# Small attention products placed crosswise in the PE array, chunk 1's tiles moved, and the third triangular solve spread over two passes

## The chip, the cores and the metric

The kernel runs on one NeuronCore of a Trainium2 chip. The metric is the device time of one execution in microseconds; the median of several runs counts. TensorE (PE in the profile) multiplies, VectorE (DVE) and ScalarE (ACT) do elementwise work and empty PSUM, GpSimd (POOL) and SyncE (SP) issue most DMAs.

## The reference

Inputs are q, k, v of shape (4, 8, 768, 48) and beta of shape (4, 8, 768), with a chain of three blocks, cut here to what is computed:

```python
k_n = k / (np.linalg.norm(k, axis=-1, keepdims=True) + 1e-06)
for t in range(S):                       # S = 768, state is 48 x 48 for each of 32 heads
    y[:, :, t] = np.einsum('bhd,bhde->bhe', q[:, :, t], state)
    v_old = np.einsum('bhde,bhd->bhe', state, kt)
    state = state + bt * np.einsum('bhd,bhe->bhde', kt, vt - v_old)
x = y.transpose(0, 2, 1, 3).reshape(3072, 384)
h = np.maximum(x @ w_in, 0.0);  x = h * h @ w_out           # w_in 384 x 2048
h = np.maximum(np.maximum(x @ w1, x @ w2), x @ w3)          # each 384 x 768
return h @ w_out2                                           # 768 x 384
```

## The kernel before

The recurrence is worked in 12 chunks of 64 tokens (C = 64). A chunk's state updates become products with the inverse X of a 64 x 64 triangular matrix for every head. The 32 heads stand as 16 pairs u; the two heads t of a pair lie in partitions 0 to 63 and 64 to 127, and the pairs fall into two halves p of 8 (U2). A product of one head contracts over its 48 or 64 partitions and writes 64 partitions, so it occupies one quarter of the array: its row half is where its inputs lie, its column half where its output lies. `half(t)` as output of head t is a diagonal quarter, `half(1 - t)` a crosswise one. In float32 one matmul of the code is two instructions in the trace.

Work of one chunk c, in `attention(c)`, is a generator whose steps are: `load_x` (X's 32 x 32 blocks into the tile xb), `scaled` and `aa` (v times a norm, pA = keys x state Sb, v -= pA), `zz` and `ww` (pZ, pW: the off-diagonal block of X), `uu` (pU = X v, copied to u), `st2` for each half (pD = state growth, pY = queries x old state plus masked products p x u, then the state is added to and pY copied to yy), and `st3` (transposes pT into X, the MoE's input). `load_att(c + 1)` issues the next chunk's DMAs on POOL: keys and queries (the tile kqs, called big in the trace), v, ktp, p. The 32 x 32 blocks are inverted for two chunks at a time by `solve32(g)`, 30 steps of two VectorE instructions each (L291, L292); the first three solves belong to chunks 0 and 1, 2 and 3, 4 and 5. `kkps` makes the products kk and p that a later solve and chunk need.

The program has a prologue (chunks 0 and 1, the first solve, the conversion of the first 12 weight tiles), six passes of the first MoE (`moe_a(P)`, chunks 2P and 2P + 1), and the second MoE. In pass P, `steps` runs 32 steps of MoE work, each a group of nine float32r products (p at L576, px at L592), and between them the steps of other generators. Lists of step numbers say when: `attention(2)` in pass 0 with [13, 13, 15, 17, ...] takes its first two steps at step 13. TensorE and VectorE keep the order in which this is written (`pin`); the prologue is ordered by the scheduler. `weights` converts a weight tile a step: a sign step (L103, L108 on ScalarE, or L103 there and L116 on VectorE), L120 on VectorE, a cast on ScalarE (L124), L128 on VectorE. gl (L583, VectorE) is the low part of a MoE group's squares; the bank p of PSUM comes free with it, and there are two such banks. Attention in the passes has the pool at, of three banks.

## Time and profile before

| | us |
|---|---|
| runs: median (lowest to highest of 3) | 955.47 (951.84 to 1011.47) |
| profiled execution, its own time | 952.68 |
| its span, first to last instruction | 951.0 |
| prologue, until the first MoE product | 83.96 |
| pass 0 | 120.21 |
| pass 1 | 95.58 |

The times of the last three lines are stretches between starts of instructions of TensorE in the profiled execution. A line of the timeline gives start, duration, engine, source line, operation, output<-inputs, shapes, and in brackets how long the engine had been idle and what ended that.

### The profile page before, as it was taken

How to read it: one execution, taken by the hardware profiler on the slowest of the kernel's cores; microseconds unless marked ns; L12 is line 12 of the kernel's file. 1: busy time of each engine (PE TensorE's matmuls, PEld its weight loads, DVE VectorE, ACT ScalarE, POOL GpSimd, SP SyncE). 2: the span in 40 equal slices, each digit the busy share in tenths (PEclk: the TensorE clock that was granted, in tenths of full speed). 3: DMA queues.
4: the chain of work that ended last, by engine and by line, in shares of the span. 5: the costliest groups of instructions: out<-in, count | busy, mean ns of one | idle time of the engine just before them, and what ended most of it. 6: DMA issues, size and time to landing. Idle time of an engine off the chain costs nothing.

```text
span 951.0 us, 23722 instructions
## 1 busy us (share of the span) xinstructions
PE 898.2 (94%) x10262; PEld 795.6 (84%) x10262; DVE 469.1 (49%) x1043; ACT 379.1 (40%) x777; POOL 136.0 (14%) x223
## 2 busy tenths in 40 slices
PE   5576988999999999999999999999999999999998
PEld 5575767777787788778878887889999999999998
DVE  5948997572574357534753333456423323323221
ACT  4526555453444344444434445665222212212211
POOL 4132003103312131213122200002000000000000
PEclk9658889799999999999999999999999999999999
DMA  9945567137614571446154303215201000000000
GB/s 270 348 122 162 170 155 176 38 113 186 153 50 127 140 168 35 133 125 151 30 153 104 108 2 116 83 59 183 66 18 50 26 26 26 17 26 10 17 18 33
DMA packets 74280, 94.92 MB, mean 100 GB/s; under 512 B 30952, under 2 KB 53256, under 8 KB 74176
## 3 DMA queue, kind: packets, MB, share of 16 engines
q1 hardware_dynamic: 55456, 54.47, 20.2%
q0 software_dynamic: 11616, 33.31, 13.1%
q10 hardware_dynamic: 7104, 5.64, 1.9%
q8 instruction: 80, 1.31, 0.6%
q14 instruction: 24, 0.20, 0.1%
HBM read 70.32 MB, written 22.64 MB: 98 GB/s over the span
## 4 chain that ended last, share of the span: by engine, by line
PE 78%; DVE 11%; DMA 4%; ACT 3%; issue 2%; POOL 0%; SPq 0%; ACTq 0%; DVEq 0%; POOLq 0%
PE p L963 24%; PE px L592 18%; PE p L576 16%; PE po L980 8%; PE pA L469 2%; DVE buf L291 2%; DVE buf L292 2%; PE pU L479 2%; PE pY L525 2%; DMA xb<-buf 1%; PE pD L496 1%; PE pZ L436 1%; PE pW L446 1%; DVE gl L583 1%; DMA big<-in_kc_dram 1%
## 5 line engine op out<-in xcount | busy, mean ns | idle before, releaser
L963 PE MATMUL p<-x_h,w 128*128 128x384 f32 x864 | 220.1, 336 | 0.0
L576 PE MATMUL p<-X,win_h 128*128 128x512 f32 x576 | 198.8, 401 | 9.8 <-DVE gl L583 8.9
L592 PE MATMUL px<-gh,wout 128*128 128x512 f32 x576 | 186.8, 406 | 0.0
L583 DVE TENSOR_TENSOR gl<-p,gh 128x512 fp32r<-128x512 f32 x96 | 66.3, 690 | 199.8 <-ACT gh L582 199.2
L963 PEld LDWEIGHTS p<-x_h,w 128*128 128x128 f32 x864 | 156.2, 188 | 0.1
L963 PE MATMUL p<-x_l,w 128*128 128x384 f32 x432 | 145.2, 336 | 0.0
L576 PEld LDWEIGHTS p<-X,win_h 128*128 128x128 f32 x576 | 110.4, 192 | 36.9 <-DVE gl L583 11.5
L580 ACT ACTIVATE p<-p 128x512 f32<-128x512 f32 x96 | 55.9, 582 | 192.6 <-PE p L576 178.5
L592 PEld LDWEIGHTS px<-gh,wout 128*128 128x128 f32 x576 | 104.5, 190 | 22.1 <-issue 0.3
L576 PE MATMUL p<-X,win_l 128*128 128x512 f32 x288 | 114.2, 397 | 0.0
L592 PE MATMUL px<-gl,wout 128*128 128x512 f32 x288 | 113.5, 394 | 0.0
L969 DVE TENSOR_TENSOR mx<-p,mx 128x384 f32<-128x384 f32 x48 | 26.7, 557 | 127.3 <-PE p L963 127.3
L963 PEld LDWEIGHTS p<-x_l,w 128*128 128x128 f32 x432 | 81.2, 188 | 0.0
L971 ACT CAST hh<-mx 128x384 fp32r<-128x384 f32 x48 | 24.6, 513 | 127.0 <-DVE mx L970 127.0
L592 PEld LDWEIGHTS px<-gl,wout 128*128 128x128 f32 x288 | 54.6, 190 | 12.1
L576 PEld LDWEIGHTS p<-X,win_l 128*128 128x128 f32 x288 | 55.3, 192 | 10.9
L292 DVE TENSOR_TENSOR buf<-buf 128x30 f32<-128x30 f32 (+9 forms) x180 | 59.7, 332 | 5.7
L291 DVE TENSOR_TENSOR buf<-buf 128x30 f32<-128x30 f32 (+9 forms) x180 | 59.1, 328 | 4.0
L582 ACT CAST gh<-p 128x512 fp32r<-128x512 f32 x96 | 56.4, 587 | 2.5
L581 ACT ACTIVATE p<-p 128x512 f32<-128x512 f32 x96 | 56.1, 584 | 2.4
L980 PE MATMUL po<-ol,hh 128*128 128x384 f32 x144 | 48.4, 336 | 0.0
L980 PE MATMUL po<-oh,hh 128*128 128x384 f32 x144 | 48.3, 337 | 0.0
(153 smaller groups left out, 1221.4 us busy)
## 6 DMA issues: line engine op xcount, KB each, us to landing
big<-in_kc_dram POOLq DMA_DIRECT2D x23, 448.0 KB, 4.9
raw<-in_moe_w_out_dram SPq DMA_DIRECT2D x22, 384.0 KB, 4.8
raw<-in_moe_w_dram SPq DMA_DIRECT2D x18, 384.0 KB, 4.5
p<-p POOLq DMA_DIRECT2D x22, 256.0 KB, 4.6
rawp<-in_moe_w_in_dram SPq DMA_DIRECT2D x12, 384.0 KB, 10.3
v<-in_vt_dram POOLq DMA_DIRECT2D x24, 192.0 KB, 3.4
ktp<-in_kt_dram POOLq DMA_DIRECT2D x24, 192.0 KB, 3.5
x<-xs SPq DMA_DIRECT2D x18, 256.0 KB, 2.6
```

Of the source, the lines that this page charges most:

```text
L291: eng.tensor_tensor(out=tv, in0=col.unsqueeze(2).broadcast_to([u, k, l]), in1=row.unsqueeze(1).broadcast_to([u, k, l]), op=ALU.mult)
L292: i = eng.tensor_tensor(out=of_, in0=of_, in1=tv, op=ALU.add)
L576: pe.matmul(p1.rearrange("p (c t) -> p c t", c=2), w[:, k, fs], x[i][k], start=n == 0, stop=n == 8)
L580: act.activation(out=p1, in_=p1, func=AF.Relu)
L581: act.activation(out=p1, in_=p1, func=AF.Square)
L582: last_gh[0] = act.copy(gh, p1).ins
L583: last_gl[0] = vec.tensor_sub(out=gl, in0=p1, in1=gh.bitcast(F32)).ins
L592: pe.matmul(px[:, k], w[:, ks], g, start=f == 0 and i == 0, stop=f == NF - 1 and i == 2, skip_group_check=True)
L963: pe.matmul(p, w[i][:, k, fs], x[:, k], start=n == 0, stop=n == 8)
L969: vec.tensor_max(out=t, in0=ps[1], in1=t)
L971: act.copy(hh[:, f], t2)
L980: pe.matmul(po[:, 0:DM], x[:, f, js], w[:, f], start=i == 0, stop=i == 17)
```

## The change

It has six parts.

1. Products of pA and pU for half 1 write to `half(t ^ p)`, crosswise, next to half 0's straight ones. What comes out crosswise has its two heads swapped, so it is emptied in two instructions of 64 partitions (`sides`). In `st2(0)` the second part of pY (`own_`) alternates with half 1's pD; in `st2(1)` pY is split in two banks, pairs 0 to 3 crosswise and 4 to 7 straight (`plain`). Chunk 0 has its own steps `state` and `ys`. For chunks 0 and 1, `ww` uses two banks.
2. Chunk 1's X is copied by VectorE and ScalarE, not by DMA; its v and p go to the tiles of the prologue's keys and are loaded earlier, ahead of ktp.
3. The matmuls `keep` on ident are added in the prologue, 24 ahead of pZ and five groups of 4.
4. `words` gives every tile that isn't signed yet its sign step on ScalarE.
5. The third solve has 12 of its steps in pass 0 and the others over steps 0 to 8 of pass 1; before, it was 24, and the rest in steps 0 to 2.
6. The step lists of attention and kkps move; in chunk 2, aa goes ahead of load_x.

```diff
-                elif c % 2:
+                elif c == 3:
                     pool.dma_start(to, own[32 * (2 * h + t):32 * (2 * h + t) + 32])
         if c < 4:
-            if c % 2 == 0:
+            if c < 3:
...
-                    if t and h:
+                    if t and (h or c < 2):
                         last_vec[0] = vec.tensor_copy(to, own[o:o + 32]).ins
...
+        sides = ((0, slice(0, 128), slice(0, 128)), (1, half(0), half(1)), (1, half(1), half(0)))
...
-                        pe.matmul(pAs[p][half(t), u], tiles[c, p][0][feat(t), u, 0], Sb[feat(t), U2 * p + u], start=True, stop=True)
-            for p in range(2):
-                v = tiles[c, p][1]
-                last_vec[0] = vec.tensor_sub(out=v, in0=v, in1=pAs[p]).ins
+                        pe.matmul(pAs[p][half(t ^ p), u], tiles[c, p][0][feat(t), u, 0], Sb[feat(t), U2 * p + u], start=True, stop=True)
+            for p, to, of_ in sides:
+                v = tiles[c, p][1][to]
+                last_vec[0] = vec.tensor_sub(out=v, in0=v, in1=pAs[p][of_]).ins
...
-                        pe.matmul(pUs[p][half(t), u], tiles[c, p][2][half(t), u], tiles[c, p][1][half(t), u], start=True, stop=True)
+                        pe.matmul(pUs[p][half(t ^ p), u], tiles[c, p][2][half(t), u], tiles[c, p][1][half(t), u], start=True, stop=True)
...
+            for p, to, of_ in sides:
+                if p and c not in (2, 3):
+                    last_vec[0] = vec.tensor_copy(us_[p][to], pUs[p][of_]).ins
                 else:
+                    last_act[0] = act.copy(us_[p][to], pUs[p][of_]).ins
...
+        plain = lambda p, u: int(p and (not c or u >= Q))
+        y_to = lambda p, u, t: pYs[p][plain(p, u)][half(t if plain(p, u) else 1 - t), u]
...
+        def past(p, u):
+            for t in range(2):
+                pe.matmul(y_to(p, u, t), tiles[c, p][0][feat(t), u, 1], Sb[feat(t), U2 * p + u], start=u == 0 or (p == 1 and u == Q), stop=False, skip_group_check=True)
+        def own_(p, u):
+            for t in range(2):
+                pe.matmul(y_to(p, u, t), tiles[c, p][3][half(t), u], tiles[c, p][7][half(t), u], start=not c and u == 0, stop=True, skip_group_check=True)
...
+        def st2(p):
+            pYs[p] = [bank([128, U2, D], "pY") for i in range(1 + p)]
+            if p:
+                for f in (past, own_):
+                    for u in range(Q):
+                        f(1, u)
+                        f(1, u + Q)
+                if c < NC - 1:
+                    added(1)
+            else:
+                for q, f in enumerate((past, own_)):
+                    if c < NC - 1:
+                        pDs[q] = bank([128, U2, D], "pD")
+                    for u in range(U2):
+                        f(0, u)
+                        if c < NC - 1:
+                            grow(q, u)
+                    if not q and c < NC - 1:
+                        added(0)
+            out_y(p)
...
-                    if f in (8, 10, 12, 14):
-                        signed(raw, last_gh[:1], True)
-                        ready = True
-                if first and not ready and f < NP:
-                    signed(raw, cast_after, True)
+                if not ready:
+                    signed(raw, [x for x in last_gh if x] or cast_after, True)
                     ready = True
...
-                extra += [([n * 3 // 2 for n in range(20)], weights(1, 1)), ([0] + [1 + n * 11 // 32 for n in range(32)], solve32(1, (pool, pool)))]
-                extra += [([13, 13, 15, 17, 18, 19, 20, 21], attention(2)), ([19, 22, 24, 25, 26, 27, 29], attention(3))]
-                extra += [([2, 3, 4, 5, 7, 8, 10, 11], kkps(HALVED[2], (at,))), ([14, 16] + [17 + n * 15 // 24 for n in range(24)], ahead_, True)]
+                extra += [([n * 3 // 2 for n in range(20)], weights(1, 1)), ([0] + [1 + n * 12 // 32 for n in range(32)], solve32(1, (pool, pool)))]
+                extra += [([10, 14, 16, 17, 18, 19, 20, 21], attention(2)), ([19, 24, 25, 26, 27, 28, 29], attention(3))]
+                extra += [([2, 3, 4, 5, 7, 8, 10, 11], kkps(HALVED[2], (at,))), ([15, 20] + [21 + n * 11 // 12 for n in range(12)], ahead_, True)]
...
-                    extra.append(([0, 0, 0, 1, 1, 1, 2, 2], ahead_))
+                    extra.append(([n * 9 // 20 for n in range(20)], ahead_))
...
-                extra += [([3, 3, 7, 9, 11, 13, 15, 17] if P > 1 else [4, 4, 9, 11, 13, 14, 16, 18], attention(2 * P + 2)), ([14, 19, 21, 23, 25, 27, 29], attention(2 * P + 3))]
+                extra += [([10, 10, 13, 14, 16, 17, 18, 19], attention(4)), ([17, 23, 24, 25, 26, 27, 29], attention(5))] if P == 1 else \
+                    [([1, 2, 6, 8, 10, 12, 14, 16], attention(2 * P + 2)), ([11, 19, 21, 23, 25, 27, 29], attention(2 * P + 3))]
```

Three places show what stands in a row on an engine. On TensorE, chunk 2's st2 in pass 0: from the end of st2(0) over a MoE group (px) to st2(1). Before:

```order
L496 MATMUL pD<-u,ktp_128 64x48 x2
L500 MATMUL pY<-Sb,big 64x48 x2
L525 MATMUL pY<-u,p 64x48 x16
L592 MATMUL px<-gh,wout_1907 128x512 x2
L592 MATMUL px<-gl,wout_1907 128x512
L592 MATMUL px<-gh,wout_1907 128x512 x2
L592 MATMUL px<-gl,wout_1907 128x512
L592 MATMUL px<-gh,wout_1907 128x512 x2
L592 MATMUL px<-gl,wout_1907 128x512
L496 MATMUL pD<-u,ktp_129 64x48 x2
L500 MATMUL pY<-Sb,big 64x48 x2
```

The same place after the change:

```order
L510 MATMUL pY<-u,p 64x48 x2
L502 MATMUL pD<-u,ktp_129 64x48 x2
L625 MATMUL px<-gh,wout_1936 128x512 x2
L625 MATMUL px<-gl,wout_1936 128x512
L625 MATMUL px<-gh,wout_1936 128x512 x2
L625 MATMUL px<-gl,wout_1936 128x512
L625 MATMUL px<-gh,wout_1936 128x512 x2
L625 MATMUL px<-gl,wout_1936 128x512
L506 MATMUL pY<-Sb,big 64x48 x16
L510 MATMUL pY<-u,p 64x48 x16
```

pD of half 1 (ktp_129) has moved ahead of the MoE group, in turn with half 0's second part of pY, and behind the group pY of half 1 stands alone.

On ScalarE, the prologue just ahead of chunk 0's pZ (xb is chunk 0's tile, xb_148 chunk 1's; buf and big take kk copies; k is written from pZ). Before:

```order
L103 ACTIVATE rawp_571<-rawp_571 128x384
L108 ACTIVATE rawp_571<-rawp_571 128x384
L858 COPY buf<-pk 128x512
L858 COPY big<-pq 128x512
L103 ACTIVATE rawp_611<-rawp_611 128x384
L108 ACTIVATE rawp_611<-rawp_611 128x384
L355 COPY xb<-buf 32x16x32 x3
L437 ACTIVATE k_271<-pZ 64x512
```

The same place after the change:

```order
L103 ACTIVATE rawp_571<-rawp_571 128x384
L108 ACTIVATE rawp_571<-rawp_571 128x384
L355 COPY xb_148<-buf 32x16x32 x2
L895 COPY buf<-pk 128x512
L895 COPY big<-pq 128x512
L103 ACTIVATE rawp_611<-rawp_611 128x384
L108 ACTIVATE rawp_611<-rawp_611 128x384
L355 COPY xb<-buf 32x16x32 x2
L438 ACTIVATE k_271<-pZ 64x512
```

Chunk 1's two copies stand ahead of the last kk copies, chunk 0's behind them.

On VectorE, the third solve at the border of passes 0 and 1 (xs<-px is the end of pass 0; the second shape of L292 names the solve's step). Before:

```order
L291 TENSOR_TENSOR buf<-buf 128x184
L292 TENSOR_TENSOR buf<-buf 128x23x8
L291 TENSOR_TENSOR buf<-buf 128x168
L292 TENSOR_TENSOR buf<-buf 128x24x7
L609 COPY xs<-px 128x512
L291 TENSOR_TENSOR buf<-buf 128x150
L292 TENSOR_TENSOR buf<-buf 128x25x6
```

The same place after the change:

```order
L291 TENSOR_TENSOR buf<-buf 128x220
L292 TENSOR_TENSOR buf<-buf 128x11x20
L291 TENSOR_TENSOR buf<-buf 128x228
L292 TENSOR_TENSOR buf<-buf 128x12x19
L642 COPY xs<-px 128x512
L291 TENSOR_TENSOR buf<-buf 128x234
L292 TENSOR_TENSOR buf<-buf 128x13x18
```

Pass 0 ends with step 12 in place of step 24.

## Rows read from the trace of the kernel before

**Rows 1.** The page: its head, and shares of the chain by engine.

```profile
span 951.0 us, 23722 instructions
...
PE 898.2 (94%) x10262; PEld 795.6 (84%) x10262; DVE 469.1 (49%) x1043; ACT 379.1 (40%) x777; POOL 136.0 (14%) x223
...
PE 78%; DVE 11%; DMA 4%; ACT 3%; issue 2%; POOL 0%; SPq 0%; ACTq 0%; DVEq 0%; POOLq 0%
```

**Rows 2.** Windows: prologue, pass 0, its first part, pass 1, pass 5.

```profile
core 0: us, PE busy (x) PEld busy (x) DVE busy (x) ACT busy (x) POOL busy (x), PEclk, DMA share, GB/s
0.00:83.96 83.96, 55.60 (x1301) 53.00 (x1301) 57.40 (x133) 36.06 (x83) 27.89 (x54) 0.72 0.82 240
83.96:204.17 120.21, 106.84 (x1454) 86.53 (x1455) 98.05 (x244) 64.67 (x136) 17.03 (x26) 0.89 0.50 132
83.96:135.77 51.81, 43.44 (x459) 33.71 (x459) 48.62 (x126) 31.61 (x66) 1.27 (x1) 0.90 0.53 153
204.17:299.75 95.58, 93.70 (x1454) 76.41 (x1453) 55.49 (x139) 40.24 (x83) 22.42 (x37) 1.00 0.45 120
580.40:646.74 66.34, 65.75 (x290) 54.13 (x289) 29.59 (x56) 41.30 (x76) 0.00 (x0) 1.00 0.30 93
```

**Rows 3.** Timeline of TensorE in pass 1, chunk 5's products.

```profile
262.11 2.07 PE L469 MATMUL pA<-Sb,big 48*64 48x48 f32 x64 [1.24 <-ACT normT L317]
264.11 0.75 PE L436 MATMUL pZ<-xb,k 32*32 32x32 f32 x64
...
280.39 0.26 PE L496 MATMUL pD<-u,ktp 64*64 64x48 f32 x2
...
281.37 1.10 PE L525 MATMUL pY<-u,p 64*64 64x48 f32 x32
282.40 0.73 PE L592 MATMUL px<-gh,wout 128*128 128x512 f32 x2
```

**Rows 4.** Timeline of TensorE in the prologue, to the first MoE product.

```profile
2.82 2.08 PE L714 MATMUL pw<-ks_more 128*128 128x128 f32 x8 [2.82 <-ACT ks_more L711]
...
45.48 1.20 PE L436 MATMUL pZ<-xb,k 32*32 32x32 f32 x64 [3.70 <-ACT xb L355]
50.86 0.28 PE L436 MATMUL pZ<-xb,buf 32*32 32x32 f32 x2 [4.18 <-DMA xb<-buf]
...
56.95 3.65 PE L479 MATMUL pU<-v,xb 64*64 64x48 f32 x64
...
83.96 0.66 PE L576 MATMUL p<-X,win_h 128*128 128x512 f32 x1 [0.93 <-ACT X L541]
```

**Rows 5.** Timeline of ScalarE and POOL: prologue, and one DMA of pass 0.

```profile
41.72 0.58 ACT L858 COPY buf<-pk 128x512 f32<-128x512 f32 x1
...
44.81 1.88 ACT L355 COPY xb<-buf 32x512 f32<-32x512 f32 x3 [1.14 <-DVE buf L323]
...
45.41 2.61 POOL L347 DMA_DIRECT2D xb<-buf  x4 [17.04 <-DVE xb L353]
...
159.15 0.54 POOL L375 DMA_DIRECT2D big<-in_kc_dram  x1 [0.81 <-DMA xb<-buf]
```

**Rows 6.** TensorE's waits in pass 0: total, times, longest.

```profile
PE p L576 <- DVE gl L583: 5.8, 2, 4.6
PE pA L469 <- DMA big<-in_kc_dram: 5.0, 1, 5.0
PE pZ L436 <- ACT xb L355: 1.4, 1, 1.4
PE pZ L436 <- DVE xb L353: 1.1, 1, 1.1
```

**Rows 7.** VectorE's groups by line in pass 0: busy us, mean ns | idle before.

```profile
L291 DVE TENSOR_TENSOR buf<-buf 128x184 f32<-128x184 f32 (+14 forms) x53 | 17.8, 336 | 0.9
...
L116 DVE TENSOR_SCALAR raw<-raw 128x384 int32<-128x384 int32 x16 | 5.4, 358 | 0.0
...
L472 DVE TENSOR_TENSOR v<-v,pA 128x384 f32<-128x384 f32 x4 | 2.0, 549 | 4.2 <-PE pA L469 4.2
```

**Rows 8.** Timeline of VectorE and TensorE in pass 1: chunk 4's inverse and pZ.

```profile
211.13 1.23 DVE L295 TENSOR_TENSOR buf<-buf,a 128x1024 f32<-128x1024 f32 x1
...
229.76 0.75 PE L436 MATMUL pZ<-xb,k 32*32 32x32 f32 x64
```

More of the change, by code (lines that the diff above doesn't have):

```diff
@@ L383, in load_att @@
         for p, us in both:
-            load(ktp[p][:, 0:U2 * D], two(kt, c, p).rearrange("p b q d -> p (b q d)"))
+            pt_ = tiles[c, p][3] = own_p.pop((c, p), None) or att.tile([128, U2, C], F32, name="p", tag="p")
+            if c:
+                pool.dma_start(pt_, p_d[c][:, us])
         yield
         for p, us in both:
-            pt_ = tiles[c, p][3] = att.tile([128, U2, C], F32, name="p", tag="p")
-            if c:
-                pool.dma_start(pt_, p_d[c][:, us])
+            load(ktp[p][:, 0:U2 * D], two(kt, c, p).rearrange("p b q d -> p (b q d)"))
+    own_v, own_p = {}, {}
     lowers, turns, last_act, last_vec = {}, {}, [None], [None]
@@ L491, in attention, with grow, added, out_y @@
         yy, pYs, pDs = {}, {}, {}
[L493 removed]
+        plain = lambda p, u: int(p and (not c or u >= Q))
+        y_to = lambda p, u, t: pYs[p][plain(p, u)][half(t if plain(p, u) else 1 - t), u]
+        def grow(p, u, swap=0):
             kt_, u_ = tiles[c, p][4], tiles[c, p][7]
             for t in range(2):
[L496 to L498 removed]
+                pe.matmul(pDs[p][half(t ^ swap), u], kt_[half(t), D * u:D * u + 64], u_[half(t), u], start=True, stop=True)
+        def past(p, u):
             for t in range(2):
[L500 to L525 removed]
+                pe.matmul(y_to(p, u, t), tiles[c, p][0][feat(t), u, 1], Sb[feat(t), U2 * p + u], start=u == 0 or (p == 1 and u == Q), stop=False, skip_group_check=True)
+        def own_(p, u):
+            for t in range(2):
+                pe.matmul(y_to(p, u, t), tiles[c, p][3][half(t), u], tiles[c, p][7][half(t), u], start=not c and u == 0, stop=True, skip_group_check=True)
+        def added(p):
+            sv = Sb[:, U2 * p:U2 * p + U2]
+            vec.tensor_add(out=sv, in0=pDs[p], in1=sv)
+        def out_y(p):
             yy[p] = att.tile([128, Q, 2, D], F32, name="yy", tag="yy")
@@ L766, in delta_moe @@
         banks[:] = [at, p1, at, p1, at]
-        kcts += [pkp.tile([R2, U2, 2, C], F32, name=f"kct{i}", tag=f"kct{i}", bufs=1) for i in range(2)]
+        keys = [pkp.tile([128, 2 * U2 * C], F32, name=f"kct{i}", tag=f"kct{i}", bufs=1) for i in range(2)]
+        kcts += [k[0:R2].rearrange("p (u t s) -> p u t s", u=U2, t=2) for k in keys]
+        for p in range(2):
+            own_v[1, p] = keys[0][:, U2 * D * p:U2 * D * (p + 1)].rearrange("p (u d) -> p u d", d=D)
+            own_p[1, p] = keys[1][:, U2 * C * p:U2 * C * (p + 1)].rearrange("p (u s) -> p u s", s=C)
         kss += [pkp.tile([128, 2, U2, C], F32, name=f"ksr{i}", tag=f"ksr{i}", bufs=1) for i in range(2)]
@@ L887, in delta_moe, with keep @@
         loads = load_att(1)
-        next(loads)
+        for _ in range(3):
+            next(loads)
         pair = [attention(0), attention(1)]
-        for n, which, ready in ((0, 0, 0), (0, 1, 0), (1, 0, 0), (0, 1, 0), (1, 0, 0), (0, 1, 0), (1, 0, 1), (1, 0, 1), (1, 1, 0), (1, 0, 1), (1, 1, 0), (1, 0, 0), (2, 1, 0), (2, 1, 0)):
+        def keep(n):
+            for _ in range(n):
+                j = pe.matmul(pw[:, 0, 0:128], ident, ident, start=True, stop=True)
+                for x in gram:
+                    behind(j.ins, x)
+        pw = ps_x2.tile([128, KD, 512], F32, name="pw", tag="px")
+        keep(24)
+        for n, which, ready, more in ((0, 0, 0, 0), (0, 1, 0, 0), (1, 0, 0, 0), (0, 1, 0, 0), (1, 0, 0, 0), (0, 1, 0, 0), (1, 0, 0, 4), (1, 0, 1, 4), (1, 0, 0, 0), (1, 1, 0, 0), (1, 0, 0, 4), (1, 1, 0, 4), (1, 1, 0, 0), (1, 1, 0, 4), (2, 1, 0, 0)):
             next(pair[which])
+            keep(more)
             if ready:
```

74 lines of the change are left out of this document (32 added, 42 removed).

## The prediction

> **What bounds the kernel now.** I read the page first: TensorE is busy for 94% of a span of 951.0 us, and 78% of the chain that ended last is TensorE's [rows 1]. So a microsecond less of TensorE's work is a microsecond less of time wherever TensorE does not wait. The windows, cut at the borders of the passes, tell where that is [rows 2]. The prologue (0 to 83.96) has TensorE busy for 55.60 us at a mean granted clock of 0.72: there the chain runs through ScalarE, VectorE and DMAs too. Pass 0 takes 120.21 us, pass 1 takes 95.58 us, with the same 1454 matmul instructions. The excess of 24.6 us is waits and, after waits, half clock (0.89 granted against 1.00). Pass 1 is TensorE's own (93.70 of 95.58 busy), and I read passes 2 to 4 as its like. Pass 5 and the second MoE, from 580.40 on, hold no attention and stay as they are.
>
> Then I read how fast the small products go [rows 3]. In pass 1, chunk 5's pA starts at 262.11 and the next work on TensorE at 264.11: 64 instructions on two quarters of the array (diagonal) in 2.00 us, 31 ns each. The interleaved pD and pY that begin at 280.39, one on the diagonal quarters, one crosswise, are 64 instructions too and end where the next product starts, 281.37: 0.98 us, 15 ns each. The 32 of pY's second part, again on two quarters, take 281.37 to 282.40, 1.03 us. So four quarters in turn cost half of two.
>
> Last, the waits: in pass 0 TensorE waits for a DMA of keys (5.0 us), for gl (5.8 us in two waits) and for chunk 2's xb (1.4 and 1.1 us) [rows 6]; in the prologue for xb (3.70 and 4.18 us) [rows 4].
>
> **The products, chunks 2 to 11.** Today a chunk has pA (64 instructions), pU (64) and pY's second part (2 x 32) on two quarters: 2.00 + 2.00 + 2.06 us. In the changed code pair half 1 of pA and pU writes crosswise beside half 0; pY's second part of half 0 runs in turn with half 1's pD, and half 1's two parts of pY are split in two banks, straight and crosswise. All then go at the four-quarter rate: 1.00 + 1.00 + 1.03, a saving of 3.0 us a chunk. Chunk 11 has no pD, and loses as much: pA 1.0, pU 1.0, half 1's pY 1.0. Ten chunks: **-30 us**, all on TensorE in stretches where it is the bound; bounds 0 (rival 2) and -30.
>
> What that adds: the crosswise half comes out with its two heads swapped, so it is evacuated in two 64-partition instructions. An evacuation of this form takes 549 ns [rows 7]; an instruction with half the partitions and the same 384 columns I take at the same price. That is +0.55 us on VectorE for pA and again for pU, per chunk, on ScalarE for pU of chunks 2 and 3. The 2.1 us of MoE products that stand between two steps cover it: VectorE is busy for 55.49 of pass 1's 95.58 us. Without that cover it would cost 1.1 us a chunk. One bank less is free after the first half's products; the next products wait for the same yy copies as today. I take 0.
>
> **The prologue.** Today chunk 1's X goes to xb1 by DMAs that POOL issues at 45.41, after it had waited 17.04 us for VectorE's copy; chunk 1's pZ starts only at 50.86, after a wait of 4.18 us for them, and pU at 56.95 [rows 4, 5]. Changed, ScalarE and VectorE copy them. ScalarE's order is now: two copies for chunk 1, two kk copies, two sign steps, two copies for chunk 0. From 44.81 that is 2 x 0.63 (a third of the 1.88 there), two kk copies and two sign steps of at most 0.58 each (the row at 41.72), and 2 x 0.63 [rows 5]: chunk 0's xb is whole at 49.2 to 49.6. VectorE's four copies and its transpose are done before. pZ of both chunks then ends at about 50.9, where chunk 1's only starts now; the hand-overs to pW and pU follow without the second wait, and pU starts at about 52.5 to 53.0. **-4 us.** The 24 added matmuls on ident stand ahead of pZ: the 8 passes of the first four took 2.08 us [rows 4], so 48 passes take 12.5 us at that rate or half of it at the clock's other level. They start when the last kk products end, about when ScalarE takes them out (41.72, [rows 5]), and end between 48 and 54.3. Behind kk products I take the first, which the wait for xb covers, at no cost, and keep +5 as a bound. The groups of four sit in waits for evacuations.
>
> From pU on there are four products on two quarters at half clock, 3.65 us each ([rows 4]: 56.95, 64 instructions): pU and pD of chunk 0, pA and pU of chunk 1. On four quarters each takes 1.83, -1.8 each, and pY -1 in all: -8 on TensorE, of which the evacuations behind them return +2.5 (three half-width instructions more on VectorE, 0.5 each, and yy of both halves on ScalarE, one after the other, +1). VectorE and ScalarE are the longer chain for part of the time, so I count -5. In sum **-9**: the first MoE product would start at 75 instead of 83.96. Bounds -3 (the added matmuls end late, evacuations take over) and -12.
>
> **Pass 0's waits.** Excess 24.6 us over pass 1, as above. Three edits work on it. (a) Third solve: 24 of its steps lie in pass 0 now, 12 then. A step is two VectorE instructions, 336 ns each [rows 7] and more for the longer ones that move, so 8 to 10 us less VectorE in pass 0. (b) All weight words get their sign step on ScalarE, in two instructions; VectorE loses L116, 16 x 358 ns = 5.4 us [rows 7], ScalarE gains about 7 in a stretch where it is busy for 64.67 of 120.21 us. (c) Places: chunk 2's xb copies come at step 14 and its pZ at step 16, where both were at 13; chunk 3's pA comes at step 24, four MoE groups after chunk 2's last read of the keys' tile, where it was two.
>
> What goes: the 5.0 us for keys, since two more MoE groups of 2.07 us (pass 5, 66.34 us for 32 steps, [rows 2]) now lie between chunk 2's last read, after which POOL issues the DMA at 159.15 [rows 5], and chunk 3's pA; the 2.5 us for xb; and the half clock after them. What stays: the first solve's prep and the weight words still stand ahead of gl in VectorE's order at the pass's start, so I keep some 3.3 of the 4.6 us there. And the second solve hardly ends sooner: from the first MoE product to chunk 2's pZ (83.96 to 135.77) VectorE is busy for 48.62 of 51.81 us [rows 2]. Less 12 of L116 (4.3), plus v of chunk 2, which is now done ahead (four or five instructions of 0.55), that is 47, or 49 with some idling. TensorE needs 16 x 2.07, four kk products and pA of about 1 each, say 40, and 43 with the wait for gl. So it waits about 6 more, somewhere. 24.6 - 3.3 - 6 is 15; with what the shorter words give, **-16**. Bounds -4 (rival 1) and -23 (pass 0 as smooth as pass 1).
>
> **Pass 1** gets the other 12 steps, spread over steps 0 to 8, so the inverse of chunk 4 is written 6 steps later than now, and chunk 4's pZ comes at step 13 instead of 9. Today the last multiplication starts at 211.13, pZ at 229.76, 18.6 us later, with no wait [rows 8]. Then, five steps with pA and a kk product, some 13 us, must hold the same chain: that multiplication, four stores, POOL's eight DMAs, their landing. Its length the trace bounds only from above. I add **+1**, bounds 0 and +4. Behind the waiting POOL DMAs is only chunk 5's load, ten us from its use.
>
> **Sum.** 951.0 - 30 - 9 - 16 + 1 = 897. The profiled execution took 952.68 us, 1.7 more than its span, and stands 2.8 below the median of 955.47 and 0.8 above the fastest run; the changed kernel's time I put at **899**.
>
> **A rule that speaks against it.** The rows from 280.39 to 281.37 [rows 3] show pD and pY, which take the same two row halves by turns, at double the rate of pA. The Trainium skill (TensorE: Matmul & The Clock Gate, Part 3: Packing small matmuls) says that LDWEIGHTS overlaps with matmuls in flight only when the row group differs. Here every third instruction shares its rows with one in flight, and by that rule a crosswise half would win nothing. The trace of before does not bear the rule out, and I give it rival 2's small chance.
>
> **Rivals.** (1) Pass 0 stays as slow as VectorE's order makes it: words, prep and second solve are the chain, and the waits only change their names. For it: VectorE is busy for 98.05 of 120.21 us [rows 2]. Against: 13 to 15 us are taken off it. Then -4 in place of -16: **911**. (2) The crosswise halves do not run beside the straight ones: -30 falls away, and the prologue gives half: **934**. Against it stand pD and pY. (3) Slower: attention's steps stand closer, and the first half's three products now hold all three banks of the pool at; if each of a chunk's three steps makes TensorE wait some 1 us for an evacuation, and the clock falls behind it, the next group takes 4.1 us for 2.07, half clock. That is 3 us x 3 x 10 = 90: 899 + 90 is about **989**. It decides where waits of 1 us drop the clock; a wait of 1.24 us ahead of 262.11 did not, pA ran at 31 ns [rows 3]. (4) Better: pass 0 becomes as smooth as pass 1, and the prologue gives 12: **889**.
>
> **Chances.** Forecast (892 to 906) 0.58, rival 1 0.2, rival 4 0.12, rival 2 0.06, rival 3 0.02, the rest unforeseen. The range reaches from rival 4's full bounds (951 - 30 - 12 - 23 + 1.7, 887) to the far side of rival 1 with pass 1's +4 and a poorer prologue, 918. Two per cent, about what a measurement of this kernel can tell from no change, is 19 us, that is 936: all but rival 3 and the worse part of rival 2 lie below. Faster 0.95, within 0.03, slower 0.02.
>
> **What would show it.** In the new profile pA and pU should last 1.0 us at full clock, a chunk's st2 no product on two quarters but chunk 11's; the first MoE product should start near 75; passes 1 to 4 should be 6.0 us shorter each; pass 0 should last 95 to 99 us, with no wait for the keys' DMA and one of about 3 us for gl near its start. Wrong would make it: a wait for xb in pass 1, evacuations of half the partitions that cost more than 0.55 us, or added matmuls that hold up pZ.

## The result, and the profile after

The changed kernel takes 958.65 us (median of 16 runs, 952.96 to 961.27), the kernel before 953.23 us (16 runs). The ratio is 1.0051, 95% interval 1.0031 to 1.0072: half a per cent slower, no change by the two per cent that the prediction names, where 899 us had been predicted. The profiled execution took 956.39 us with a span of 954.7. The page of the changed kernel, its head, busy times and chain, answers to [rows 1]:

```profile
span 954.7 us, 23942 instructions
...
PE 879.3 (92%) x10350; PEld 774.7 (81%) x10350; DVE 475.4 (50%) x1032; ACT 395.3 (41%) x816; POOL 132.0 (14%) x219
...
PE 70%; DVE 9%; DMA 8%; ACT 6%; issue 3%; SPq 2%; POOL 1%; DVEq 0%; ACTq 0%; POOLq 0%
```

TensorE is busy for 18.9 us less, although it has 88 more instructions. But its share of the chain fell from 78% to 70%, and DMAs and ScalarE took that share: TensorE now waits where it worked. The windows of the changed kernel, cut at the first MoE product of each pass (columns as in [rows 2]), show where:

```profile
0.00:88.39 88.39, 59.23 (x1389) 55.27 (x1389) 57.99 (x131) 41.41 (x97) 25.38 (x50) 0.75 0.78 228
88.39:203.97 115.58, 95.51 (x1454) 76.43 (x1455) 84.34 (x198) 74.49 (x161) 16.56 (x26) 0.93 0.48 135
203.97:306.93 102.96, 92.13 (x1454) 73.76 (x1453) 65.85 (x163) 40.42 (x83) 22.50 (x37) 0.95 0.42 112
306.93:402.71 95.78, 91.01 (x1454) 73.54 (x1453) 52.97 (x125) 40.36 (x83) 22.54 (x37) 0.96 0.47 120
402.71:500.47 97.76, 92.33 (x1454) 74.36 (x1453) 53.01 (x125) 40.34 (x83) 22.54 (x37) 0.95 0.43 108
500.47:584.12 83.65, 82.66 (x1133) 67.14 (x1132) 33.47 (x65) 43.21 (x86) 15.52 (x26) 1.00 0.33 83
```

Pass 1 had TensorE busy for 93.70 of 95.58 us; now it is busy for 92.13 of 102.96, so some 11 us of it is idle, and part of the rest runs at a lower clock (0.95 granted, 1.00 before). Pass 0 is 4.6 us shorter, far from the 95 to 99 us foreseen. Of passes 1 to 4 only pass 4, the one without a solve and without key products, became clearly shorter: 88.81 to 83.65 us, at full clock.

TensorE's timeline in pass 1 of the changed kernel, chunk 5, answers to [rows 3]:

```profile
271.63 1.15 PE L473 MATMUL pA<-Sb,big 48*64 48x48 f32 x64
272.71 0.75 PE L437 MATMUL pZ<-xb,k 32*32 32x32 f32 x64
...
280.97 1.08 PE L448 MATMUL pW<-k,xT 32*32 32x32 f32 x64 [5.21 <-DVE xT L430]
281.98 0.80 PE L609 MATMUL p<-X,win_h 128*128 128x512 f32 x1
```

pA starts at 271.63, the next product at 272.71: 64 instructions in 1.08 us instead of 2.00. The spreading does what it says. Then pW waits 5.21 us, and the MoE products behind it start at half clock (granted clock 0.50 from 278.23 to 285.06). VectorE's timeline of the same kernel tells why:

```profile
277.39 0.40 DVE L292 TENSOR_TENSOR buf<-buf 128x234 f32<-128x234 f32 x1
277.71 1.02 DVE L464 TENSOR_TENSOR v<-v,normT 128x384 f32<-128x384 f32 x2
278.65 1.70 DVE L476 TENSOR_TENSOR v<-v,pA 128x384 f32<-128x384 f32 x3
280.38 0.45 DVE L430 STREAM_TRANSPOSE xT<-x 128x256 f32<-128x256 f32 x1
```

pA had ended at 272.7, but its evacuation (L476) starts only at 278.65: up to 277.8 VectorE goes through steps of the fourth solve, 0.4 us an instruction (L291, L292), which stand ahead of it in its order. xT follows behind, and pW needs xT. TensorE's waits in pass 0 (first four lines, answering to [rows 6]) and in pass 1 (total, times, longest):

```profile
PE pq L183 <- DVE v L476: 8.7, 1, 8.7
PE p L609 <- DVE gl L616: 3.8, 1, 3.8
PE pY L506 <- ACT yy L524: 3.2, 2, 1.6
PE pk L183 <- DVE buf L200: 1.7, 1, 1.7
...
PE pW L448 <- DVE xT L430: 5.2, 1, 5.2
PE pD L502 <- issue: 3.3, 1, 3.3
PE pZ L437 <- DMA xb<-xt: 1.3, 1, 1.3
```

In pass 0 the waits for the keys (5.0) and for xb (2.5) are gone and the gl wait is 3.8, near the forecast; a wait of 8.7 us for v, an evacuation of pA, has come. The 3.3 us in pass 1 that the view puts down to "issue" are a wait for chunk 4's u, by VectorE's timeline and TensorE's:

```profile
252.01 1.23 DVE L237 TENSOR_TENSOR buf<-buf,r 128x1024 f32<-128x1024 f32 x1
...
254.79 1.12 DVE L487 COPY u<-pU 64x384 f32<-64x384 f32 x2
...
256.01 0.26 PE L502 MATMUL pD<-u,ktp 64*64 64x48 f32 x2 [3.26 <-issue]
```

The copy of u (L487) stands behind the fourth solve's preparation (up to L237, the norms and scaling ahead of its steps) and its first steps, and pD starts when it is done.

In the prologue, ScalarE's and TensorE's timelines of the changed kernel:

```profile
41.28 0.56 ACT L103 ACTIVATE raw<-raw 128x384 f32<-128x384 f32 x1 [13.52 <-DMA raw<-in_moe_w_out_dram]
41.73 0.55 ACT L108 ACTIVATE raw<-raw 128x384 int32<-128x384 uint16 x1
42.17 0.57 ACT L895 COPY ksr<-pk 128x512 f32<-128x512 f32 x1
...
49.60 5.62 PE L928 MATMUL pw<-ident 128*128 128x128 f32 x48
55.16 1.20 PE L437 MATMUL pZ<-xb,k 32*32 32x32 f32 x64
...
88.39 0.50 PE L609 MATMUL p<-X,win_h 128*128 128x512 f32 x1 [0.92 <-ACT X L572]
```

ScalarE waits 13.52 us for the first w_out tile, whose sign step stands ahead of the copies of the key products (L895). The fillers (the `keep` matmuls on ident), ordered behind the key products, start at 49.60 instead of some 42, and pZ behind them at 55.16.

### The profile page after: what moved, and what is told of

The parts are those of the page before. It is cut to its first block, busy times and chain, and to the rows that moved or that the text cites. A ratio compares the mean times of both kernels' runs of the same rounds, so it can differ in the third digit from the quotient of the medians.

```text
span 954.7 us, 23942 instructions
## 1 busy us (share of the span) xinstructions
PE 879.3 (92%) x10350; PEld 774.7 (81%) x10350; DVE 475.4 (50%) x1032; ACT 395.3 (41%) x816; POOL 132.0 (14%) x219
## 4 chain that ended last, share of the span: by engine, by line
PE 70%; DVE 9%; DMA 8%; ACT 6%; issue 3%; SPq 2%; POOL 1%; DVEq 0%; ACTq 0%; POOLq 0%
PE p L1009 24%; PE p L609 15%; PE px L625 14%; PE po L1026 8%; DMA raw<-in_moe_w_out_dram 2%; DMA buf<-kk 2%; DVE buf L291 1%; DVE buf L292 1%; DMA xb<-xt 1%; PE pU L483 1%; SPq L93 1%; ACT p L613 1%; PE pW L448 1%; ACT p L614 1%; PE pw L928 1%
## 5 line engine op out<-in xcount | busy, mean ns | idle before, releaser
L609 PE MATMUL p<-X,win_h 128*128 128x512 f32 x576 | 201.0, 405 | 5.3 <-DVE gl L616 4.4
L625 PEld LDWEIGHTS px<-gh,wout 128*128 128x128 f32 x576 | 107.0, 191 | 24.4 <-ACT wout L124 1.5
L1015 DVE TENSOR_TENSOR mx<-p,mx 128x384 f32<-128x384 f32 x48 | 26.7, 557 | 127.3 <-PE p L1009 127.3
L292 DVE TENSOR_TENSOR buf<-buf 128x30 f32<-128x30 f32 (+9 forms) x180 | 59.6, 331 | 5.8
L291 DVE TENSOR_TENSOR buf<-buf 128x30 f32<-128x30 f32 (+9 forms) x180 | 59.1, 328 | 4.2
```

Source lines behind the costliest of these rows:

```text
L291: eng.tensor_tensor(out=tv, in0=col.unsqueeze(2).broadcast_to([u, k, l]), in1=row.unsqueeze(1).broadcast_to([u, k, l]), op=ALU.mult)
L292: i = eng.tensor_tensor(out=of_, in0=of_, in1=tv, op=ALU.add)
L609: pe.matmul(p1.rearrange("p (c t) -> p c t", c=2), w[:, k, fs], x[i][k], start=n == 0, stop=n == 8)
L625: pe.matmul(px[:, k], w[:, ks], g, start=f == 0 and i == 0, stop=f == NF - 1 and i == 2, skip_group_check=True)
L1015: vec.tensor_max(out=t, in0=ps[1], in1=t)
```

## The experiments

**Theory A**: the spread products earn what was predicted, and the moved steps lose it again, because VectorE and ScalarE work in order. **Theory B**: the spreading itself brings the waits, by evacuations in halves and by three banks held at once. Every kernel is read by its stages, since a wait belongs to one of them. A stage ends at the first MoE product of the next pass; pass 5 (66.3 us) and all behind it (304.2 us) are the same in all kernels. Lengths in us, from one profiled execution each; the ratio is to the kernel before in the same session:

| kernel | prologue | pass 0 | 1 | 2 | 3 | 4 | ratio (95%) |
|---|---|---|---|---|---|---|---|
| before | 83.96 | 120.21 | 95.58 | 96.19 | 95.65 | 88.81 | 1 |
| after | 88.39 | 115.58 | 102.96 | 95.78 | 97.76 | 83.65 | 1.0051 (1.0031-1.0072) |
| spread_only | 81.73 | 113.44 | 91.65 | 94.30 | 93.55 | 83.32 | 0.9745 (0.9719-0.977) |
| no_sign | 81.45 | 116.91 | 103.09 | 97.83 | 97.17 | 83.22 | 0.9979 (0.996-0.9997) |
| old_steps | 85.83 | 112.38 | 91.96 | 94.91 | 93.06 | 83.39 | 0.9784 (0.9763-0.9806) |
| spread_early | 82.86 | 114.75 | 92.50 | 97.50 | 92.96 | 83.26 | 0.9782 (0.9762-0.9803) |
| with_solve3 | 82.33 | 112.47 | 98.65 | 95.19 | 91.91 | 83.39 | 0.9839 (0.9804-0.9874) |
| with_keys | 82.13 | 113.84 | 95.15 | 100.36 | 98.10 | 83.33 | 0.9957 (0.9938-0.9975) |
| with_att | 82.54 | 114.57 | 97.97 | 99.71 | 96.22 | 83.74 | 0.9901 (0.9874-0.9928) |
| with_pass0 | 82.34 | 123.27 | 91.73 | 94.91 | 92.02 | 83.33 | 0.988 (0.9856-0.9904) |
| pass0_late_pA | 83.04 | 118.39 | 91.41 | 97.11 | 93.55 | 83.26 | 0.9816 (0.9771-0.9861) |
| pass0_chunk3 | 82.58 | 116.47 | 91.61 | 95.31 | 91.92 | 83.39 | 0.9808 (0.9772-0.9844) |
| solve3_wide5 | 83.18 | 111.70 | 100.13 | 96.23 | 91.94 | 83.39 | 0.9847 (0.9806-0.9888) |
| sign_pass0 | 83.16 | 111.76 | 92.01 | 94.30 | 91.91 | 83.33 | 0.9758 (0.9709-0.9806) |
| early_no_keep | 80.59 | 114.26 | 92.69 | 95.31 | 92.09 | 83.27 | 0.9737 (0.9695-0.9778) |
| after_no_keep | 81.62 | 116.54 | 103.54 | 98.23 | 96.34 | 83.30 | 1.0012 (0.9989-1.0035) |
| keys_earlier | 82.79 | 114.66 | 91.97 | 90.57 | 90.40 | 83.27 | 0.9681 (0.9628-0.9734) |
| best | 80.12 | 115.50 | 92.22 | 90.20 | 90.29 | 83.39 | 0.9688 (0.9647-0.973) |

How far a stage moves by itself is seen where kernels share its code. The nine with spread_only's prologue lie at 81.7 to 83.2; after and old_steps, whose prologues have the same code, lie 2.6 apart (ScalarE got the w_out tile at 41.28 and 39.88). Pass 0 lies at 113.4 to 114.7 in the four that have it alike, pass 1 at 91.4 to 92.7 in eight, pass 3 at 91.9 to 93.6 and pass 2 at 94.3 to 97.5 in ten. With all lists of the change (after, no_sign, after_no_keep) pass 1 lies at 103.0 to 103.5, pass 2 at 95.8 to 98.2, pass 3 at 96.3 to 97.8. Smaller differences than these are not read.

**Which part loses.** spread_only has the crosswise products, with their evacuations and banks, in the code of the kernel before:

```diff
-pe.matmul(pAs[p][half(t), u], ...)
+pe.matmul(pAs[p][half(t ^ p), u], ...)
```

> The kernel before with the crosswise products alone: its step lists, its prologue, its sign steps and its third solve stay, so that only the products' halves, the half-width evacuations and the two banks of the second output differ. Theory A (the spreading earns its time, the moved steps around it lose it again): pass 4, in which no solve and no key products run, fell from 88.80 to 83.65 us in the changed kernel, 5.15 us for two chunks; five such pairs of chunks and some 2 us of chunk 1 in the prologue make 27 us less, 926 us, ratio 0.972. Theory B (the spreading itself brings the waits, by half-width evacuations that stand in VectorE's and ScalarE's order and by three attention banks held at once): the waits of 3 to 5 us in passes 1 to 3 stay, and the time is 948 us or more, ratio 0.995 or above.

930.23 us: A, by most of its size. Chunks 2 to 11 gain, pass 4 alone 5.5 us.

no_sign takes the sign step (edit 4) out of the changed kernel.

> The changed kernel with the words' sign step put back where it was (on VectorE with a shift for most tiles, on ScalarE for four tiles of w_out and the first twelve of w_in). Theory A: ScalarE no longer waits 13.5 us in the prologue for the first w_out tile's DMA with the copies of the key products behind it; the first MoE product comes near 79 us instead of 88.4, and the time is 949 us, ratio to the kernel before 0.996. In pass 0 VectorE gets some 30 shifts back, which could cost up to 5 us of that. Theory B (the prologue's loss is the filler products and the order of its chain, not the sign step): the first MoE product stays at 86 us or later, 956 to 959 us, ratio 1.003 or above.

952.73 us: the first MoE product comes at 81.45, so the sign step costs the prologue 6.9 us there. The first 24 fillers then start at 41.35, as the prediction had it, and pZ waits for xb all the same. The time lies between the two theories, since passes 1 to 3 stay as long as in the changed kernel and pass 0 is 1.3 us longer. old_steps takes the lists and the split solve (edits 5 and 6) out instead:

```diff
-([1, 2, 6, 8, 10, 12, 14, 16], attention(2 * P + 2)), ([11, 19, ...
+([3, 3, 7, 9, 11, 13, 15, 17] if P > 1 else [4, 4, 9, ...
```

> The changed kernel with the step lists of the kernel before (attention, key products, second and third solve, the third solve whole in pass 0, chunk 2's first product after its load); the spreading, the prologue's edits and the sign steps stay. Theory A: the waits of passes 0 to 3 for VectorE (8.7 us of the key products for v, 7.0 us of pA for X, 5.2 us for xT, 3.3 us for u) go, passes 1 to 3 are some 5 us shorter each than before, and pass 0 is no longer than 120 minus 3: 958.7 - (102.96 - 90.5) - (95.78 - 91) - (97.76 - 90.5) + 2 = 936 us, ratio 0.982. Theory B (the waits come with the spreading): they stay in other places, 950 us or more, ratio 0.997 or above.

934.24 us, theory A, and spread_early, without edits 4, 5 and 6:

> The changed kernel with both the step lists and the sign steps of the kernel before: what is left is the spreading, chunk 1's early tiles and copies, and the filler products. Theory A: both losses go, the first MoE product comes at 75 to 79 us, passes 1 to 4 are 5 us shorter than before: 953 - 27 - 6 = 920 us, ratio 0.965. Theory B (the spreading's own waits, and a prologue held by its filler products): 945 us or more, ratio 0.991 or above.

934.88 us, between the theories' 920 and 945: passes 1 to 4 are near spread_only's, but the prologue gains nothing. So the lists and the split solve cost some 24 us, more than all else, and chunk 1's early tiles with the fillers bring nothing.

**Which list.** Each group of the lists was put on spread_only alone. First the split third solve, with the later steps of pass 1 that it needs:

```diff
-([0, 0, 0, 1, 1, 1, 2, 2], ahead_)
+([n * 9 // 20 for n in range(20)], ahead_)
```

> The spread-only kernel (930.2 us; prologue 81.7, passes 113.4, 91.7, 94.3, 93.6, 83.3, 66.3) with one thing of the change more: the third solve runs on into pass 1, and pass 1's attention steps move back with it (to steps 10 to 29). Theory A (the solve's steps stand in VectorE's order ahead of what attention's products wait for): pass 0 is 2 to 4 us shorter, pass 1 is 8 to 11 us longer, with waits of pD for u and pW for xT; 936 us, ratio to the kernel before 0.980. Theory B (the losses of pass 1 come from the key products' later steps): pass 1 stays within 2 us of 91.7, 927 us, ratio 0.971.

936.30 us, theory A, if smaller: pass 1 is 7.0 us longer with a wait of 4.4 us of pW for xT, pass 0 shorter by 1.0, about its scatter. Then the key products:

```diff
-([3, 4, 5, 6, 8, 9, 10, 11], kkps(...)), ([12, 14] + ...
+([2, 3, 4, 5, 7, 8, 11, 12], kkps(...)), ([13, 15] + ...
```

> The spread-only kernel with the key products' last two steps at 11 and 12 and the later solves at 13, 15 and 16 to 30 (passes 1 to 3). Theory A: the solve's preparation waits for the late store and load of the key products and stands in VectorE's order ahead of X; each of passes 2 and 3 has a wait of 3 to 4 us of pA or of another product for VectorE and is 2 to 4 us longer, 935 us, ratio 0.980. Theory B (the wait needs the earlier attention steps, in which chunk 2P+3's first product stands at step 11): 930 us, ratio 0.974, no wait over 2 us in passes 2 and 3.

947.16 us, more than either theory gave: pass 2 is 6.1 us longer, pass 3 4.6. VectorE's timeline of with_keys in pass 2, then TensorE's:

```profile
341.24 0.19 DVE L246 COPY ss<-buf 128x32 f32<-128x32 f32 x1 [3.17 <-DMA buf<-kk]
...
344.58 1.23 DVE L237 TENSOR_TENSOR buf<-buf,r 128x1024 f32<-128x1024 f32 x1
...
345.81 0.55 DVE L514 TENSOR_TENSOR Sb<-pD,Sb 128x384 f32<-128x384 f32 x1
...
346.42 0.90 PE L569 MATMUL pT<-ident,yy 128*128 128x128 f32 x3 [5.54 <-DVE Sb L514]
```

The preparation (L246 to L237) waits 3.17 us for the reload of the key products, then works for 4.6. The addition to the state, whose bank pT needs, stands behind all of it: TensorE waits 5.54 us. Theory B, that the earlier attention steps are needed for a wait, is out. Those attention steps alone:

> The spread-only kernel with the attention steps of the change in passes 1 to 4 (chunk 2P+2 from step 1, chunk 2P+3's first product at step 11; pass 1 at 10 and 17), the solves and key products where they were. Theory A as for the key products' steps: attention's steps alone meet the preparation at 12 to 14 and cost 0 to 2 us a pass; pass 1, all of whose attention moves back 6 steps, loses 2 us; 934 us, ratio 0.978. Theory B (the earlier first product of chunk 2P+3 is what waits): waits of 3 to 4 us of pA for X in passes 2 and 3, 938 us, ratio 0.983.

943.25 us, again more than either theory gave. Its waits in pass 1 and pass 2:

```profile
PE pW L448 <- DVE xT L430: 4.4, 1, 4.4
...
PE pT L569 <- DVE Sb L514: 5.5, 1, 5.5
```

pT waits the same 5.5 us for Sb in pass 2, and pass 1 takes 97.97 with the same 4.4 us of pW for xT, without a split solve. With the split solve beside it (with_solve3) pass 1 takes 98.65, 0.7 more, within the scatter: the split by itself costs nothing that can be read. The two lists together cost less (pass 2: 95.78, against 100.36 and 99.71): in the changed kernel the key products and attention moved in step, and what was left in its passes 2 and 3 is a wait of pA for X, behind the preparation:

```profile
PE pA L473 <- DVE X L573: 3.2, 1, 3.2
...
PE pA L473 <- DVE X L573: 3.9, 1, 3.9
```

Pass 0's lists:

> The spread-only kernel with the change's steps of pass 0 for attention and the second solve, chunk 2's first product at step 10 ahead of its load; the third solve stays whole in pass 0. Theory A (the first product's pA takes two of three banks while VectorE, behind the second solve, can't empty them): the key products wait some 8 us for VectorE's v, pass 0 is 4 to 8 us longer than 113.4 though the keys' wait of 1.7 to 5 us goes; 936 us, ratio 0.980. Theory B (that wait needs the sign step on ScalarE or the third solve's shorter list): pass 0 is 0 to 3 us shorter, 928 us, ratio 0.972.

Pass 0 is 9.8 us longer, theory A and somewhat more. TensorE's row of with_pass0, and VectorE's around it:

```profile
125.80 0.37 PE L183 MATMUL pq<-big 48*64 48x64 f32 x2 [8.38 <-DVE v L476]
...
124.07 0.27 DVE L292 TENSOR_TENSOR buf<-buf 128x108 f32<-128x108 f32 x1
124.26 1.02 DVE L464 TENSOR_TENSOR v<-v,normT 128x384 f32<-128x384 f32 x2
125.20 1.69 DVE L476 TENSOR_TENSOR v<-v,pA 128x384 f32<-128x384 f32 x3
```

The second solve's steps run up to 124.3; then v is scaled, and the key product starts when the first subtraction has read pA's bank.

**Within the lists.** pass0_late_pA keeps those lists but leaves chunk 2's pA behind its load, at step 14 instead of 10:

> The spread-only kernel with the change's steps of pass 0, but chunk 2's first product stays behind its load at steps 13 and 14 and not ahead of it at step 10. With the product at step 10 pass 0 took 123.3 us, without any of these steps 113.4. Theory A (the early pA is the cause: it takes banks that the key products' next tile waits for, until VectorE, behind the second solve, has read them): the wait of 8.4 us for v goes and pass 0 takes 113 to 117 us; 932 us, ratio 0.977. Theory B (the later steps of chunk 3 and of the second solve cost it): pass 0 stays at 120 us or more, 937 us or more, ratio 0.984.

Pass 0 takes 118.39: neither theory in full. The wait for v is gone, 4.9 of the 9.8 us are the early pA. pass0_chunk3 has chunk 3's list alone (24, 25, 26 for 22, 24, 25):

> The spread-only kernel with chunk 3's steps of pass 0 alone as in the change: 19, 24, 25, 26, 27, 28, 29 instead of 19, 22, 24, 25, 26, 27, 29. Theory A (of the 5 us that the change's pass 0 costs beside its early pA, the one-step gap ahead of chunk 3's pW makes the most): a wait of 2 to 3 us of pW for VectorE's xT comes, pass 0 takes 116 to 118 us, 934 us, ratio 0.980. Theory B (chunk 2's steps and the second solve's later end cost it): 112 to 115 us, 930 us, ratio 0.975.

```profile
173.67 1.92 PE L448 MATMUL pW<-k,xT 32*32 32x32 f32 x64 [2.68 <-DVE xT L430]
```

That row of TensorE is theory A: 3.0 us in pass 0. What is left, 1.9, is near the scatter. In pass 1 the same cure was tried: chunk 5 back at 14, 19, 21, beside the split solve.

> The spread-only kernel with the third solve run on into pass 1, chunk 4's attention steps moved back as in the change, but chunk 5's steps as in the kernel before, with two steps between its products (14, 19, 21, 23, 25, 27, 29) instead of one (17, 23, 24, 25, 26, 27, 29). With the latter pass 1 took 98.7 us with a wait of 4.4 us of pW for xT; the kernel with chunk 5's and 4's later steps but without the split solve had the same wait and 98.0. Theory A (one step between chunk 5's first product and pW is too short for VectorE's v, v and xT behind the solve's steps): the wait falls under 1.5 us, pass 1 takes 91 to 95 us, 931 us, ratio 0.976. Theory B (the split solve or chunk 4's later steps cost it): 97 us or more, 936 us, ratio 0.982.

In this kernel chunk 5's load at step 14 overwrites the shared xb ahead of chunk 4's pU, so chunk 4's output is computed with another factor; the work is the same. The wait for xT is gone, but pA now waits for X, by the view of waits in its pass 1:

```profile
PE pA L473 <- DVE X L573: 4.3, 1, 4.3
```

Pass 1 takes 100.13. Of theory A only the wait for xT held; the wider gap does not shorten pass 1. Chunk 5's pA now stands directly behind chunk 4's output, and on VectorE the addition into X (L573, at 255.59) stands behind a gl that waited 3.93 us for ScalarE and behind four solve instructions. Whether another place for chunk 5 would do better was not tried.

**The prologue.** early_no_keep is spread_early without the fillers:

> The change without its step lists, its sign steps and its filler products: the spreading, and chunk 1's early tiles and copies. The same with the filler products had its first MoE product at 82.9 us, the spread-only kernel at 81.7. Theory A (the fillers cost about what they give back in clock, and the early tiles save little since the key products of the second pair end the chain): first MoE product at 81 to 84 us, 931 to 935 us, ratio 0.975 to 0.979. Theory B (the fillers hold up pZ, which waits for nothing else): first MoE product at 79 us or earlier, 930 us or less, ratio 0.974. Theory C (the fillers keep TensorE's clock up, and without them the prologue's products run at half clock): 86 us or later, 937 us.

80.59 us, between theories A and B, and at 928.77 us a time that theory B gave. But B's mechanism is out: pZ starts at 48.18 without the fillers and at 48.05 with them. So is theory C: the mean granted clock of the prologue falls from 0.79 to 0.66, and yet the prologue is not longer. The fillers cost 2.3 us there, not far above the scatter. after_no_keep takes them (44 matmuls in the code, 88 instructions) from the changed kernel:

> The changed kernel without its 48 filler products, all else as changed. Theory A (the prologue's loss needs both: the sign step holds ScalarE's copies of the key products 13.5 us for a DMA, so the key products end at 49.6 us, and the first 24 fillers, ordered behind them, then hold pZ 5.5 us more): the first MoE product comes at 82 to 84 us instead of 88.4, 953 us, ratio 1.000. Theory B (the late copies alone delay everything behind them): 86 us or later, 956 to 959 us, ratio 1.004.

81.62 instead of 88.39: theory A. The late copies alone cost 1.0 us (81.62 against 80.59), no more than the scatter, the fillers behind them 6.8. And sign_pass0 has the sign step in pass 0 alone, as its text says; but the first one is ordered by nothing and again went ahead of the copies (a wait of 13.89 us):

> The spread-only kernel with the words' sign step on ScalarE in pass 0 alone; the prologue keeps its order. Theory A (the sign step off VectorE helps pass 0, which VectorE bounds, and only its place in the prologue's order loses time): the prologue stays at 82 us, the waits of the first products for gl and of pA for the keys shrink, pass 0 is 1.5 to 4 us shorter than 113.4; 927 us, ratio 0.972. Theory B (ScalarE's extra 0.5 to 1 us steps stand ahead of the evacuations that attention's products wait for): pass 0 as long or longer, 930 us or more, ratio 0.974 or above.

929.97 us: prologue and pass 0 lie 1.4 above and 1.7 below spread_only, within or near the scatter, so the sign step gives nothing measurable.

**Better versions.** keys_earlier moves the key products the other way, to 2, 3, 4, 5, 7, 8, 9, 10 and the solve's loads to 11:

> The spread-only kernel with the key products one or two steps earlier in passes 1 to 3 (steps 2 to 10 where they stood at 3 to 11) and the solve's loads started at step 11 instead of 12; its preparation stays at 14. Theory A (the preparation's first instruction waits 3.0 us for the reload of the key products and holds VectorE's and ScalarE's later evacuations): the wait goes, the wait of pY for ScalarE's yy (1.3 us a pass) too, passes 2 and 3 are 1.5 to 3 us shorter; 926 us, ratio 0.971. Theory B (the preparation's own 4.5 us of VectorE work is what holds them, or the attention steps alone): 929 to 932 us, ratio 0.975 to 0.977.

925.18 us, ratio 0.9681. Passes 2 and 3 are 5.6 and 5.3 us shorter than before. ScalarE, VectorE and TensorE in pass 2, spread_only's timeline:

```profile
331.31 0.19 DVE L246 COPY ss<-buf 128x32 f32<-128x32 f32 x1 [3.01 <-DMA buf<-kk]
...
331.53 0.23 ACT L219 ACTIVATE s<-ss 128x32 f32<-128x32 f32 x1 [4.42 <-DVE ss L246]
331.79 1.29 ACT L524 COPY yy<-pY 64x192 f32<-64x192 f32 x4
...
333.13 0.61 PE L506 MATMUL pY<-Sb,big 48*64 48x48 f32 x26 [1.30 <-ACT yy L524]
```

and VectorE's in keys_earlier:

```profile
330.17 0.19 DVE L246 COPY ss<-buf 128x32 f32<-128x32 f32 x1 [1.04 <-DMA buf<-kk]
```

In spread_only the square root of the preparation (L219) waits with it and holds yy, an evacuation, on ScalarE; that is where st2(1) found no bank. In keys_earlier the reload is waited for 1.04 us, and pY no longer waits; a wait of pA for a key product's copy (1.2 us) went too.

best adds early_no_keep and a sign step in pass 0 that is ordered behind the prologue:

> What helped put together: the spreading, chunk 1's early tiles and copies without fillers, the words' sign step on ScalarE in pass 0 alone and its first one ordered behind the prologue's last ScalarE step, the key products of passes 1 to 3 one or two steps earlier; all else in the steps of the kernel before. If the stages add up as each was measured: prologue 80.6, pass 0 112, pass 1 92, passes 2 and 3 90.5 each, pass 4 83.3, pass 5 66.3, the rest 304.2: a span of 919.5 us and a time of 921 us, ratio 0.967. If the sign step in pass 0 gives nothing, 923 us, ratio 0.968; if a new wait comes with the parts together, 926 us or more, ratio 0.972.

923.52 us, ratio 0.9688, what was expected if the sign step gives nothing, and no better than keys_earlier: the prologue is 80.12, pass 0 is 115.50 where 112 was hoped for. Both beat both kernels by 3%.

## Why the prediction was wrong, point by point

Of the 57.7 us between the span of 897 that was summed up and the 954.7 measured, 26.9 lie in passes 1 to 4 (23 shorter forecast, 3.9 longer measured), 17.4 in pass 0 (22 shorter forecast, its two chunks' products included; 4.6 measured) and 13.4 in the prologue (9 shorter forecast, 4.4 longer measured).

**The products, -30: mechanism right, size nearly.** pA takes 1.08 us, pass 4 is 5.2 us shorter (6.0 forecast). In keys_earlier the prologue and passes 0 to 4 together are 26.7 us shorter. **Half-width evacuations** cost what was taken, 1.70 us for three. "I take 0" held in pass 4, and in passes 2 and 3 once the preparation was out of their way; behind it, spread_only lost some 3.5 of 5.5 us in each. Cover was counted by VectorE's busy share of a pass; it has to be counted by what stands ahead in its order at that step.

**The step that failed** is edit 6, the moved step lists, most of all in passes 1 to 4. There its lists were never costed: "passes 1 to 4 should be 6.0 us shorter each" takes the moved steps as free, and **pass 1, +1**, weighs only chunk 4's xb, which did wait (1.3 us, within its bounds). Against spread_only the lists and the split solve cost 11.3 us in pass 1 and 4.2 in pass 3, by waits for VectorE, behind the solve and its preparation, and the half clock after them; in pass 2 the 1.5 us more lie within the scatter, but keys_earlier, with the key products moved the other way, has 5.2 us less there. VectorE is busy in pass 1 for no more than 65.85 of 102.96 us. The Trainium skill (Perfetto Trace Analysis, Identifying the Most-Contended Engine) says to use an engine's occupancy to find the bottleneck. By that measure VectorE, 64% busy, is not the one in pass 1 of this trace, and yet it is the engine that TensorE waits for longest.

**Pass 0's waits, -16: measured +2.1.** The products alone bring pass 0 to 113.44 (spread_only, 6.8 less than before, where two chunks' products were to give 6.0); the changed kernel has 115.58. The gains are there in kind: the waits for keys and xb went, gl's is 3.8. But of the new places the early pA (+4.9) and chunk 3's steps (+3.0) were not priced, though the text said that TensorE would wait "about 6 more, somewhere". The VectorE time of (a) and (b), 13 to 15 us, bought 7.7 (123.27 to 115.58): with fewer solve steps in pass 0 chunk 3's wait for xT is 0.2 us in the changed kernel, while the 8.7 us behind the early pA stayed.

**The prologue, -9: measured +4.4.** Copies: -4 forecast, -0.6 measured, by TensorE's timeline of early_no_keep (56.95 before):

```profile
48.18 1.92 PE L437 MATMUL pZ<-xb,k 32*32 32x32 f32 x64 [6.99 <-ACT xb L355]
...
56.31 1.96 PE L483 MATMUL pU<-v,xb 64*64 64x48 f32 x64
```

Both pZ end at 51.8, near the 50.9 foreseen; but then pW of both chunks takes 4.5 us to pU, where the text allowed about 2. Products behind pU: -5 forecast, -2.7 measured (24.3 us for 27.0). Fillers and sign step: 0 forecast, +7.8 (80.59 to 88.39; 5.2 by old_steps' 85.83). The fillers' start was placed at 41.72, and the sign step of the first w_out tile, which the new code leaves without order, was not looked for on ScalarE.

**The rivals.** Rival 2 is out: pA's 64 instructions go at 17 ns each, for 31 before. The Trainium skill (TensorE: Matmul & The Clock Gate, Part 3: Packing small matmuls) says that weight loads overlap with running matmuls only where the row group differs. The row halves alternate alike in both kernels and the rate nearly doubled, so that rule does not set the rate here. Rival 1's "the waits only change their names" is what pass 0 did in part. Rival 3 named what came, "attention's steps stand closer", waits for evacuations and half clock behind them, and had a chance of 0.02. Its other half, the three banks, fits waits of pY for yy that the kernel before does not have: 1.9 and 1.3 us in spread_only's passes 0 and 2, 3.2 us in pass 0 of the changed kernel. Its price of 90 us was for every step of a chunk; what came against spread_only is 26.1 us to the end of pass 5 (650.45 and 624.33), at a few steps and in the prologue.

Pass 1's 11.3 us: the later attention steps alone cost 6.3 (with_att), the split on top of them 0.7 (with_solve3), the key products' steps alone 3.5 (with_keys), in sum 10.5. What stays open: in passes 2 and 3 the lists don't add up like this, and no run shows why each costs more alone than both together; nor was each chunk's list in them tried apart. A small slip in the prediction, on which nothing hangs: 16 x 358 ns is 5.7 us, and 5.4 is the row's own busy time.

## What to carry to other kernels

When an edit moves steps, write down for each in-order engine what now stands ahead of every evacuation that the next product waits for, above all instructions that wait for a DMA; its busy share does not tell. Price each list apart, stage by stage: here one good edit (ratio 0.9745 by itself) hid in a bundle that measured as nothing. Work that fills a wait must be ordered behind nothing that can come late.
